# Packed rows loaded for two blocks by one transfer, maxima's transfers posted first, and mid-heads operand loads moved and spread, in a four-layer attention and Fourier network

## The chip, the cores and the metric

The kernel runs on one core of a Trainium2 chip. Its time is the device time of one execution in microseconds (us); for several runs the median is given. A core has five engines that work through their own instructions in order: PE (TensorE, matrix products; its weight loads are listed apart as PEld), DVE (VectorE), ACT (ScalarE), POOL (GpSimd) and SP (SyncE). Here SP issues every transfer (DMA), one after the other, and a transfer that has to wait holds up all that are behind it in SP's queue.

## The reference

Four layers are applied to x of 2048 rows by 640 columns: attention, Fourier, attention, Fourier.

```python
x = x + A(layernorm(x));  x = x + B(layernorm(x));  x = x + A(layernorm(x));  x = x + B(layernorm(x))
# A: 32 heads of 20 columns, sliding window of 256 keys, softmax, then @ wo
# B: Real(DFT over the sequence of (DFT over the columns))
```

All is float32; products are made from a high and a low part of each operand, three matrix products for one.

## The kernel before

**Heads stage.** The change lies in the attention layers, in `heads` (lines 522 to 743) and what it calls. Eight quads of four heads are worked through, each over 16 blocks of 128 rows. The loop runs over steps -10 to 128. In step t the scores of block s = t + 10 are made twice: first as rows, to find each row's maximum (`s_head`, PE L553, masked and reduced by DVE at L558), and ten steps later, for block t, transposed (`t_head`, PE L583, with the maximum subtracted by an extra row of the operand), exponentiated by ACT (L592) and masked by POOL (`t_mask`, L598 and L602). `pv` (PE L613) of block t - 1 comes at the end of step t and needs the masks of step t - 1. A step has two halves, z = 0 and z = 1.

**Maxima.** After each four blocks `m_rows` transposes their maxima (PE L565), ACT negates them into `mt` (L567), and two transfers (L569) put them into the extra rows of `qp`. That is at the end of every fourth step (86, 90, 94, 98); the first `t_head` that reads them comes at the start of the fourth step after it.

**Fill.** In the first half of each step PE also gets `fill`: matrix products for other parts of the layer (L191), first those that project x to queries and keys (`project`, `pieces`), and when these are done, the early part of the output projection (`partials`), which covers three of five operand chunks. 16 row tiles of it take two steps each. `more()` gives no fill while the first set of these operands, `early_o[0]`, is not complete. What is not done when the loop ends is done after it, at first tile by tile in `late`.

**Ticks.** Work on other engines that belongs to a later time is posted: `post(n, f)` runs f in the n-th tick from now, and each half step ends with a tick. Post 0 runs in the same tick as post 1, but before all that was posted for it. `defer(n, f)` runs f at the start of the n-th step from now. All this orders the program text only; what the engines do in time follows from their queues.

**Projected pieces.** A finished projection piece (128 columns of queries and keys, called chunk c, over 512 rows) is copied by ACT (L477), split by POOL (L478, L479) one and two ticks later, and stored to DRAM (`qk_d`, 512 KB) by `store_qk` (L456) six ticks after the copy. The last chunk is the tenth.

**Packed rows.** `pack(quad, sb)` loads a quad's rows from `qk_d` into `qp` and `kp` with 12 transfers of 20 rows by two groups by 512 columns (80 KB each, L510). It runs for four blocks at a time, eight steps ahead of their `s_head`, and three transfers go out at the start of each of four steps.

**Softmax sums.** `pv` also gives each row's sum. `finish` (L626 to L640) works on four finished blocks: at ticks 2, 12 and 14 it loads the sums back (`sm`, L631) and stores the outputs (L632), takes the reciprocal on DVE (L634) and stores it (L637).

**Early operands.** `prepare(2)` runs in step 84. It loads the first operand of the output projection (heads 0 to 15, chunk 0) by `load_o` (L759, and L765 for its scale). `others` waits, from step to step, until the reciprocals of quad 5's first four blocks are stored, and then loads the other two. Seven ticks after its load an operand is scaled by POOL (L782), four ticks later it is cut in two parts by ACT and POOL (L160, L166), and with the next tick it counts as complete. `prepare(4)`, after the last projection piece, in step 92, loads the first four row tiles of x (`load_y`, L853), one in each step. The sums of `partials` are added to them by DVE (L877).

Of the kernel before, what the change touches and what calls it, by code (L numbers as in the profile page):

```python
# [23 lines left out]
NQ = H // 4  # L24
NSB = 4
NB = S // P
NCH = 2 * D // P
# [36 lines left out]
class Net:  # L64
# [394 lines left out]
    def pieces(self, c, sbs, role):  # L459

        w = self.turn["w", c]
        sets, of = [], {}
        for sb in sbs:
            xt = self.xnt(sb)
            if sb % 2 == 0:
                sets.append(([], []))
            p = self.bank(role)
            of[id(p)] = p, sb, self.last_bank
            sets[-1][0].append(p)
            sets[-1][1].append([((w[:, 0, k, :], w[:, 1, k, :]), (xt[:, 0, k, :], xt[:, 1, k, :])) for k in range(KC)])  # L470

        lead = self.lead

        def copied(p, sb):
            st = self.work.tile([P, 2, 512], F32R, name="c", tag="c", bufs=3)
            r = self.raw()[:, :512]
            self.nc.scalar.activation(r, p, AF.Copy)  # L477
            self.post(1, lambda: self.nc.gpsimd.tensor_copy(st[:, 0, :], r))  # L478
            self.post(2, lambda: self.nc.gpsimd.tensor_tensor(  # L479
                out=st[:, 1, :], in0=r, in1=st[:, 0, :].bitcast(F32), op=OP.subtract))  # L480
            self.post(3 if lead else 6, lambda: self.store_qk(c, sb, st))
        for r in self.lockstep(sets):
            if isinstance(r, tuple):
                for p in r[1]:
                    p, sb, k = of[id(p)]
                    self.heavy.append((k, lambda p=p, sb=sb: copied(p, sb)))
                r = 0
            yield r
# [12 lines left out]
        self.prepare(4)  # L501


    def pack(self, quad, sb):

        todo = []
        cols = slice(sb * 512, (sb + 1) * 512)

        def put(d, src):
            self.nc.sync.dma_start(d.bitcast(F32), src)  # L510

        for kind in (1, 0):
            for e in range(2):
                r0 = 160 * quad + 80 * kind + 40 * e
                dst = (self.qp, self.kp)[kind][quad % 2].rearrange("p (z s) -> p z s", z=2)
                for part, l in enumerate(((0, 1, 0), (0, 0, 1))[kind]):
                    b = 64 * e + 20 * part
                    src = self.qk[l, r0:r0 + 40, cols].rearrange("(z r) s -> r z s", z=2)
                    todo.append(lambda d=dst[b:b + 20, :, cols], src=src: put(d, src))
        return todo  # L520

    def heads(self, xsrc, xdst, hook):
# [7 lines left out]
        def defer(d, fn):  # L530
            later.setdefault(now[0] + d, []).append(fn)
# [30 lines left out]
        def m_rows(quad, u):  # L562
            m = mc.pop((quad, u))
            p = self.banks[:16, s_bank(), :P]
            nc.tensor.transpose(p, m.rearrange("p z e j -> p (z e j)"), self.ident)  # L565
            mt = pool.tile([16, P], F32R, name="mt", tag="mt", bufs=1)
            nc.scalar.activation(mt, p, AF.Copy, scale=-1.0)  # L567
            for z in range(2):
                self.post(1, lambda z=z: nc.sync.dma_start(  # L569
                    qp[quad % 2][60:125:64, z, u * 512:(u + 1) * 512].bitcast(F32),  # L570
                    mt[8 * z:8 * z + 8, :].bitcast(F32)))

# [53 lines left out]
        def finish(quad, bk, ou):  # L626
            sm = pool.tile([P, 16], F32, name="sm", tag="sm")
            rc = pool.tile([P, 16], F32, name="rc", tag="rc")
            cols = slice(bk * 512, (bk + 1) * 512)
            at = (2, 12, 14) if quad < NQ - 1 else (1, 5, 6)  # L630
            self.post(at[0], lambda: nc.sync.dma_start(sm, ou[0:P:32, :]))  # L631
            self.post(at[0], lambda: nc.sync.dma_start(  # L632
                self.od[4 * quad:4 * quad + 4, :, cols].rearrange("h r s -> (h r) s"), ou))
# [2 lines left out]
            def store():  # L636
# [7 lines left out]
        done = [2 * NSB * per_piece]  # L644

        due = [(16 * q + 4 * j - AHEAD, ((-(-160 * (q + 1) // P) - 1) * NSB + 2 * (j // 2) + 2) * per_piece)
               for q in range(1, NQ) for j in range(NSB)]
        self.xsrc = xsrc
        self.out = self.partials(xsrc)
        self.rest = self.late(xsrc, xdst, hook)  # L650
# [44 lines left out]
        for step in range(-LEAD, steps + 1):  # L695
# [5 lines left out]
            if due and s >= due[0][0]:  # L701
                while done[0] < due[0][1]:
                    fill(15)
                due.pop(0)
                q, j = (s + AHEAD) // 16, (s + AHEAD) % 16 // 4
                for i, f in enumerate(self.pack(q, j)):
                    defer(i // 3, f)
                for f in later.pop(step, []):
                    f()
            if v >= 0 and v % 4 == 3:  # L710
# [100 lines left out]
    def prepare(self, n):  # L811
# [9 lines left out]
        elif n == 2:  # L821
# [11 lines left out]
            def others():  # L833

                if (CHUNKS[EARLY - 1][1] // 4 - 1, 0) not in self.stored:
                    self.defer(1, others)
                    return
                for k in range(1, EARLY):
                    self.early_o[0]["left"] -= 1
                    self.load_o(self.early_o[0], 0, k)  # L840
            self.defer(1, others)
        elif n == 4:
            self.take_big(2, F32)
            for i in range(AHEAD_X):
                if i == 0:
                    self.load_y([i])
                else:
                    self.defer(i, lambda i=i: self.load_y([i]))

    def load_y(self, ts):  # L850
        for t in ts:
# [878 lines left out]
```

## Time and profile before

| what | us |
|---|---|
| median of 3 runs (lowest, highest) | 2174.63 (2174.54, 2177.93) |
| the profiled execution: its own time | 2173.64 |
| its span, first to last instruction | 2171.9 |
| busy in the span: PE, DVE, ACT, POOL | 2116.4, 1611.6, 1167.9, 932.6 |
| first and last `s_head`, first attention layer to second | 125.0 to 1570.0 |
| mean granted clock of PE (1 is full) | 0.997 |

The profile is taken by the hardware from one execution. In its rows, "out<-in" names the tiles that an instruction writes and reads, L583 is line 583 of the kernel, and a bracket such as [0.44 <-POOL pt L598] is the idle time of the engine before the instruction with what ended it. A list of waits gives the engine and line that waited, what for, the total, the number of times and the longest. A queue name with a q (SPq) is the sequencer of that engine, which issues transfers. Engines that are not the bottleneck may idle for nothing.

### The profile page before, as it was taken

To read this page: it belongs to the slowest core of one execution; us is meant where nothing else is said; L and a number is where in the kernel's file an instruction comes from. 1 tells how busy PE (TensorE), PEld (TensorE's weight loads), DVE (VectorE), ACT (ScalarE), POOL (GpSimd) and SP (SyncE) were. 2 spreads that over 40 slices of the span, in tenths; PEclk is the share of its full clock that TensorE was granted. 3 is DMA by queue.
4 is the path that set the end of the run, shared out by engine and by line. 5 is a ranking of instruction groups with operands and counts; after the bars stand their busy time and mean duration, and the time that the engine had idled before them with its cause. 6 is when DMAs were issued, how large, how long until landed. Compare 5 with 4: busy or idle time off the path is not lost.

```text
span 2171.9 us, 49261 instructions
## 1 busy us (share of the span) xinstructions
PE 2116.4 (97%) x17893; PEld 1768.5 (81%) x17893; DVE 1611.6 (74%) x3933; ACT 1167.9 (54%) x2611; POOL 932.6 (43%) x1458
## 2 busy tenths in 40 slices
PE   7999999899999999999999999998999999999999
PEld 7987777687878888889999877776777788888899
DVE  6348888786897968787751578887768878688777
ACT  3117887766554545543431288786665545455522
POOL 3037777876514224230230477777754333242300
PEclk9999999999999999999999999999999999999999
DMA  5546666786435353657646466667853454546653
GB/s 184 177 146 198 203 190 212 218 233 200 135 122 180 132 187 126 224 196 258 214 140 189 152 201 187 207 193 224 233 184 130 130 189 136 165 148 218 221 176 125
DMA packets 221619, 395.41 MB, mean 182 GB/s; under 512 B 39360, under 2 KB 85952, under 8 KB 221376
## 3 DMA queue, kind: packets, MB, share of 16 engines
q1 hardware_dynamic: 221376, 392.26, 57.0%
q8 instruction: 141, 2.31, 0.5%
q14 instruction: 102, 0.84, 0.1%
HBM read 273.94 MB, written 117.05 MB: 180 GB/s over the span
## 4 chain that ended last, share of the span: by engine, by line
PE 81%; DVE 6%; POOL 4%; ACT 4%; DMA 3%; issue 2%; SPq 0%; ACTq 0%; POOLq 0%; DVEq 0%
PE banks L1269 27%; PE banks L173 14%; PE banks L191 13%; PE banks L613 8%; PE banks L1524 6%; PE banks L583 6%; PE banks L553 4%; POOL ou L1199 1%; POOL big L166 1%; DVE qp L166 1%; ACT big L931 1%; PE banks L273 1%; PE banks L565 1%; POOL rs L981 1%; ACT big L160 1%
## 5 line engine op out<-in xcount | busy, mean ns | idle before, releaser
L558 DVE CUSTOM_DVE_ANT_0 banks<-banks,mask 128x384 f32<-128x384 f32 (+2 forms) x1024 | 525.5, 559 | 153.4 <-PE banks L553 117.5
L592 ACT ACTIVATE pt<-banks 128x384 f32<-128x384 f32 (+2 forms) x1024 | 430.1, 472 | 139.8 <-PE banks L553 59.5
L583 PE MATMUL banks<-qp,kp 61*128 61x384 f32 (+2 forms) x1024 | 302.8, 365 | 9.7 <-DMA qp<-mt 7.7
L598 POOL TENSOR_SCALAR_AFFINE_SELECT pt<-pt 128x256 f32<-128x256 f32 x512 | 213.5, 418 | 174.9 <-ACT pt L592 128.4
L553 PE MATMUL banks<-kp,qp 60*128 60x384 f32 (+2 forms) x1024 | 279.1, 359 | 4.8 <-DVE mc L558 4.5
L191 PE MATMUL banks<-big,wc 64*128 64x512 f32 x1920 | 272.1, 394 | 0.4 <-DVE pt L374 0.4
L583 PEld LDWEIGHTS banks<-qp,kp 61*128 61x128 f32 x1024 | 176.8, 185 | 68.0 <-issue 27.4
L613 PE MATMUL banks<-pt,vq 128*32 128x128 f32 x5760 | 215.3, 277 | 4.4 <-POOL pt L598 4.4
L191 PEld LDWEIGHTS banks<-big,wc 64*128 64x128 f32 x1920 | 183.3, 185 | 29.1 <-ACT x L477 6.7
L613 PEld LDWEIGHTS banks<-pt,vq 128*32 128x32 f32 x5760 | 144.3, 109 | 65.2 <-issue 48.2
L1199 POOL TENSOR_TENSOR pt<-pt,pt 128x512 f32<-128x512 f32 x36 | 62.8, 1744 | 293.0 <-DMA pt<-c 188.3
L602 POOL TENSOR_SCALAR_AFFINE_SELECT pt<-pt 128x256 f32<-128x256 f32 x448 | 187.4, 418 | 0.0
L553 PEld LDWEIGHTS banks<-kp,qp 60*128 60x128 f32 x1024 | 163.7, 185 | 26.7 <-DVE mc L558 16.3
L160 ACT ACTIVATE c<-pt 128x512 fp32r<-128x512 f32 x150 | 93.5, 626 | 151.0 <-POOL pt L1175 52.4
L160 ACT ACTIVATE qp<-pt 128x512 fp32r<-128x512 f32 (+1 forms) x195 | 119.9, 624 | 92.2 <-DVE pt L1200 38.9
L166 DVE TENSOR_TENSOR c<-pt,c 128x512 fp32r<-128x512 f32 x150 | 125.0, 843 | 52.0 <-ACT c L160 49.8
L166 DVE TENSOR_TENSOR qp<-pt,qp 128x512 fp32r<-128x512 f32 (+1 forms) x195 | 150.2, 783 | 12.4 <-ACT qp L160 9.8
L1269 PE MATMUL banks<-qp,big 128*128 128x512 f32 x630 | 151.2, 391 | 4.9 <-DVE qp L166 3.9
L558 DVE DVE_READ_ACCUMULATOR2_ANT mc<- 128x1 f32 x1024 | 145.2, 142 | 0.0
L1269 PEld LDWEIGHTS banks<-qp,big 128*128 128x128 f32 x630 | 117.0, 188 | 31.0 <-DVE qp L166 5.6
L1269 PE MATMUL banks<-qp,xc 128*128 128x512 f32 x480 | 117.9, 390 | 1.5 <-DVE xc L166 1.2
L1269 PEld LDWEIGHTS banks<-qp,xc 128*128 128x128 f32 x480 | 89.8, 188 | 21.9 <-DVE xc L166 2.1
(224 smaller groups left out, 4388.6 us busy)
## 6 DMA issues: line engine op xcount, KB each, us to landing
pt<-c SPq DMA_DIRECT2D x188, 512.0 KB
qk_d<-c SPq DMA_DIRECT2D x80, 512.0 KB
kp<-qk_d SPq DMA_DIRECT2D x384, 80.0 KB
qp<-qk_d SPq DMA_DIRECT2D x384, 80.0 KB
kp<-u_d SPq DMA_DIRECT2D x32, 640.0 KB
o_d<-ou SPq DMA_DIRECT2D x64, 256.0 KB
x_d<-x SPq DMA_DIRECT2D x48, 320.0 KB
v_d<-pt SPq DMA_DIRECT2D x16, 768.0 KB
```

The source lines that it names most:

```text
L160: nc.scalar.activation(hi, src, AF.Copy, scale=-1.0 if neg else 1.0)
L166: (eng or nc.vector).tensor_tensor(out=lo, in0=src, in1=hi.bitcast(F32), op=OP.subtract)
L173: self.nc.tensor.matmul(p, x, y, start=n == 0, stop=n == last)
L191: self.nc.tensor.matmul(ps[a], x[r], y[r], start=half + i == 0, stop=half == 1 and i == n - 1, skip_group_check=True)
L553: nc.tensor.matmul(p, qp[quad % 2][b:b + 60, z, qb * P:(qb + 1) * P], kp[quad % 2][b:b + 60, z, k0 * P:(qb + 1) * P], start=True, stop=True)
L558: nc.vector.tensor_tensor_reduce(out=p, in0=p, in1=self.mask[:, 384 - n * P:], scale=1.0, scalar=NEG, op0=OP.add, op1=OP.max, accum_out=mc ...
L583: nc.tensor.matmul(self.banks[:, tb[e], :n * P], kp[quad % 2][b:b + 61, z, kb * P:(kb + 1) * P], qp[quad % 2][b:b + 61, z, kb * P:(kb + n) ...
L592: nc.scalar.activation(pt[quad, kb][:, 2 * z + e, :n * P], self.banks[:, tb[e], :n * P], AF.Exp, scale=SCALE)
L598: nc.gpsimd.affine_select(out=t[:, :, 0:P], in_=t[:, :, 0:P], pattern=[[0, 2], [1, P]], compare_op=OP.is_ge, fill=0.0, base=0, channel_mul ...
L602: nc.gpsimd.affine_select(out=t[:, :, 256:384], in_=t[:, :, 256:384], pattern=[[0, 2], [-1, P]], compare_op=OP.is_gt, fill=0.0, base=0, ch ...
L613: nc.tensor.matmul(p[32 * h:32 * h + 32, :], vq[:, 96 * (kb % 4) + 21 * h:96 * (kb % 4) + 21 * h + 32], t[:, h, (qb - kb) * P:(qb - kb + 1 ...
L1269: nc.tensor.matmul(self.banks[:, bk, :], p, b[q], start=start and m == 0, stop=stop and last and m == 2, skip_group_check=True)
```

## The change

Six edits, all of them in the heads stage of both attention layers:

- `pack` takes a number of quarters; in the loop it loads two (1024 columns, 160 KB a transfer), at the first and third of the four times, two transfers at the start of each of six steps.
- The maxima's transfers are posted with 0 instead of 1.
- The last chunk's pieces are stored eight ticks after their copy, not six.
- For quad 5's first four blocks the reciprocal and its store come at ticks 8 and 9, not 12 and 14.
- The second early operand is loaded three steps after `prepare(2)`; the third by `others`, which begins to look four steps after it, not one.
- The first four row tiles of x are loaded one, three, five and seven steps after `prepare(4)`, not zero to three.

```diff
--- before.py
+++ after.py
@@ -478,7 +478,7 @@
             self.post(1, lambda: self.nc.gpsimd.tensor_copy(st[:, 0, :], r))
             self.post(2, lambda: self.nc.gpsimd.tensor_tensor(
                 out=st[:, 1, :], in0=r, in1=st[:, 0, :].bitcast(F32), op=OP.subtract))
-            self.post(3 if lead else 6, lambda: self.store_qk(c, sb, st))
+            self.post(3 if lead else 6 if c < NCH - 1 else 8, lambda: self.store_qk(c, sb, st))
         for r in self.lockstep(sets):
             if isinstance(r, tuple):
                 for p in r[1]:
@@ -501,10 +501,10 @@
         self.prepare(4)
 
 
-    def pack(self, quad, sb):
+    def pack(self, quad, sb, n=1):
 
         todo = []
-        cols = slice(sb * 512, (sb + 1) * 512)
+        cols = slice(sb * 512, (sb + n) * 512)
 
         def put(d, src):
             self.nc.sync.dma_start(d.bitcast(F32), src)
@@ -566,7 +566,7 @@
             mt = pool.tile([16, P], F32R, name="mt", tag="mt", bufs=1)
             nc.scalar.activation(mt, p, AF.Copy, scale=-1.0)
             for z in range(2):
-                self.post(1, lambda z=z: nc.sync.dma_start(
+                self.post(0, lambda z=z: nc.sync.dma_start(
                     qp[quad % 2][60:125:64, z, u * 512:(u + 1) * 512].bitcast(F32),
                     mt[8 * z:8 * z + 8, :].bitcast(F32)))
 
@@ -628,6 +628,8 @@
             rc = pool.tile([P, 16], F32, name="rc", tag="rc")
             cols = slice(bk * 512, (bk + 1) * 512)
             at = (2, 12, 14) if quad < NQ - 1 else (1, 5, 6)
+            if (quad, bk) == (CHUNKS[EARLY - 1][1] // 4 - 1, 0):
+                at = (2, 8, 9)
             self.post(at[0], lambda: nc.sync.dma_start(sm, ou[0:P:32, :]))
             self.post(at[0], lambda: nc.sync.dma_start(
                 self.od[4 * quad:4 * quad + 4, :, cols].rearrange("h r s -> (h r) s"), ou))
@@ -644,7 +646,7 @@
         done = [2 * NSB * per_piece]
 
         due = [(16 * q + 4 * j - AHEAD, ((-(-160 * (q + 1) // P) - 1) * NSB + 2 * (j // 2) + 2) * per_piece)
-               for q in range(1, NQ) for j in range(NSB)]
+               for q in range(1, NQ) for j in range(0, NSB, 2)]
         self.xsrc = xsrc
         self.out = self.partials(xsrc)
         self.rest = self.late(xsrc, xdst, hook)
@@ -703,8 +705,8 @@
                     fill(15)
                 due.pop(0)
                 q, j = (s + AHEAD) // 16, (s + AHEAD) % 16 // 4
-                for i, f in enumerate(self.pack(q, j)):
-                    defer(i // 3, f)
+                for i, f in enumerate(self.pack(q, j, 2)):
+                    defer(i // 2, f)
                 for f in later.pop(step, []):
                     f()
             if v >= 0 and v % 4 == 3:
@@ -835,17 +837,17 @@
                 if (CHUNKS[EARLY - 1][1] // 4 - 1, 0) not in self.stored:
                     self.defer(1, others)
                     return
-                for k in range(1, EARLY):
-                    self.early_o[0]["left"] -= 1
-                    self.load_o(self.early_o[0], 0, k)
-            self.defer(1, others)
+                other(EARLY - 1)
+
+            def other(k):
+                self.early_o[0]["left"] -= 1
+                self.load_o(self.early_o[0], 0, k)
+            self.defer(3, lambda: other(1))
+            self.defer(4, others)
         elif n == 4:
             self.take_big(2, F32)
             for i in range(AHEAD_X):
-                if i == 0:
-                    self.load_y([i])
-                else:
-                    self.defer(i, lambda i=i: self.load_y([i]))
+                self.defer(1 + 2 * i, lambda i=i: self.load_y([i]))
 
     def load_y(self, ts):
         for t in ts:
```

## The prediction

> **What bounds the kernel now.** I read the page first (TensorE, PE, is busy for 97% of the span, so only the other 55 us can go), then the list of who waited for whom on PE, then a table of windows through the second attention layer, then the chain and the timeline where a window stood out. The waits on PE that the change can touch are two:
>
> ```profile
> PE banks L583 <- DMA qp<-mt: 7.7, 2, 4.8
> PE banks L613 <- POOL pt L598: 4.4, 7, 1.1
> ```
>
> Columns are total us, times, longest. The first is the exponent pass waiting for the maxima's transfer, once in each attention layer. The windows (bounds, length, then busy us of PE, PE's loads, DVE, ACT, POOL, then PE's clock, DMA share, GB/s) show an ordinary stretch, and those around the waits:
>
> ```profile
> 300.00:310.00 10.00, 10.00 (x149) 7.52 (x139) 7.10 (x32) 8.39 (x23) 9.77 (x20) 1.00 0.62 193
> 420.00:430.00 10.00, 6.59 (x68) 5.22 (x68) 5.14 (x21) 5.42 (x15) 7.27 (x14) 0.83 0.80 254
> 1490.00:1500.00 10.00, 8.51 (x117) 5.14 (x117) 8.28 (x32) 6.71 (x21) 8.00 (x18) 1.00 1.01 266
> 1500.00:1510.00 10.00, 5.18 (x51) 4.44 (x49) 3.18 (x14) 3.87 (x11) 4.89 (x9) 0.66 0.76 240
> ```
>
> In an ordinary stretch PE is full: fewer or later transfers there cannot shorten it, only lengthen it. Around the waits PE is idle, its granted clock drops, and the DMA engines are full (share 1.01) just before. The chain of work through that place in the second layer (start, us, what) goes through GpSimd (POOL) first and the maxima afterwards:
>
> ```profile
> 1486.16 1.27 POOL c L479
> 1487.43 0.55 POOL c L478
> 1487.98 0.37 POOL pt L598
> 1488.35 0.36 POOL pt L602
> 1488.71 1.27 POOL c L479
> 1489.97 0.37 POOL pt L598
> ...
> 1499.42 5.30 DMA qp<-mt
> ...
> 1510.22 1.32 PE banks L191 x18
> ```
>
> The timeline gives the steps (the first L583 of each) and both waits:
>
> ```profile
> 426.35 0.66 PE L583 MATMUL banks<-qp,kp 61*128 61x384 f32 x1 [2.87 <-DMA qp<-mt]
> 430.88 0.44 PE L583 MATMUL banks<-qp,kp 61*128 61x384 f32 x1
> 434.07 0.44 PE L583 MATMUL banks<-qp,kp 61*128 61x384 f32 x1
> 1493.27 0.32 PE L583 MATMUL banks<-qp,kp 61*128 61x128 f32 x1
> 1493.42 0.27 ACT L567 ACTIVATE mt<-banks 16x128 fp32r<-16x128 f32 x1
> 1495.59 0.44 PE L583 MATMUL banks<-qp,kp 61*128 61x384 f32 x1
> 1498.05 0.44 PE L583 MATMUL banks<-qp,kp 61*128 61x384 f32 x1
> 1504.86 0.66 PE L583 MATMUL banks<-qp,kp 61*128 61x384 f32 x1 [4.82 <-DMA qp<-mt]
> ```
>
> Counted from the stage's start these begin steps 98, 99, 100 of the first layer and 95, 96, 97, 98 of the second. The maxima of step 94 are ready at 1493.69, but SyncE's queue (SP) issues them only at 1499.42; the other transfers stand ahead of them there:
>
> ```profile
> 1488.02 1.33 SPq L759 DMA_DIRECT2D x<-o_d  x2
> 1492.31 0.34 SPq L853 DMA_DIRECT2D big<-x_d  x1
> 1495.15 0.37 SPq L456 DMA_DIRECT2D qk_d<-c  x1
> 1496.66 0.32 SPq L853 DMA_DIRECT2D big<-x_d  x1
> 1497.54 1.05 SPq L510 DMA_DIRECT2D kp<-qk_d  x3
> 1498.93 0.39 SPq L456 DMA_DIRECT2D qk_d<-c  x1
> ...
> 1501.41 0.35 SPq L853 DMA_DIRECT2D big<-x_d  x1
> ```
>
> **The change, part by part** (base: the profiled execution, 2173.64 us, of which 2171.9 are the span; the median of the runs is 0.99 higher).
>
> *Maxima first, loads and stores spread: the wait goes.* Post 0 runs in the same tick as post 1, only ahead of the others there. So it passes just the store in front (0.39 us of issue); most must come from the rest. Steps 92 and 93 lose both row loads (6 of 80 KB), step 92 its two operand loads and one scale load (768 KB), three of four x loads move behind step 94, and the last chunk's stores (512 KB each) fall behind the maxima. From step 92 to the maxima some 1.1 MB are issued instead of 3.6 MB, in a longer time. I take the whole wait as gone: -2.87 and -4.82.
>
> *Half clock after it.* Step 98 took 4.53 us in the first layer (426.35 to 430.88), the next, with the same work at full clock, 3.19. That is -1.34 in each layer with the wait. The Trainium skill ("TensorE: Matmul & The Clock Gate", Part 1) says the clock falls to half after an idle window of about 3.4 us and asks for no gap over about 3 us. Here the 2.87 us gap was followed by a window at 0.83, so the trace is stricter; by the page the first layer's 1.34 would not come from the wait, and the gain would be that much smaller.
>
> *Operands earlier: fill from step 95.* Scale values of quad 5 are stored at post 9 instead of 14, at the end of step 88 instead of in step 91. Operand 1 is loaded in step 87, operand 2 in step 89, both in 92 before. Scaling follows 7 ticks after a load, cutting 4 later, and the fill may start one tick after that: in step 95, not 98. Three steps without fill (95 to 97: 2.32 + 2.46 + 1.99, the last up to the wait) become three with fill at 3.19: +2.8. Each brings half a partial product forward, so that three late tiles run in the loop's last steps instead of behind it. Behind it one takes 1.70, as these two rows stand apart:
>
> ```profile
> 527.76 1.15 PE L173 MATMUL banks<-qp,kp 128*128 128x320 f32 x6 [0.42 <-DVE x L970]
> 529.45 1.14 PE L173 MATMUL banks<-qp,kp 128*128 128x320 f32 x6 [0.54 <-DVE x L970]
> ```
>
> That is -5.1; in the loop each takes the place of a fill of 18 matmuls (1.32 on the chain above), for which I charge the difference, 0.4, three times: +1.2. Net -1.1 (bounds 0, if Fourier's start is tied to something else, and -2).
>
> *The same operands on POOL.* Before, the scaling of two operands (step 95) and their cutting (step 97) were bursts of 2.5 us that cost PE nothing; POOL had idled before them:
>
> ```profile
> 1483.96 0.41 POOL L598 TENSOR_SCALAR_AFFINE_SELECT pt<-pt 128x256 f32<-128x256 f32 x1 [0.45 <-ACT pt L592]
> 1488.68 1.29 POOL L479 TENSOR_TENSOR c<-x,c 128x512 fp32r<-128x512 f32 x1
> 1490.39 0.41 PE L613 MATMUL banks<-pt,vq 128*32 128x128 f32 x4 [0.44 <-POOL pt L598]
> 1494.78 2.51 POOL L782 TENSOR_TENSOR x<-x,rr 128x512 f32<-128x512 f32 x2
> 1500.32 2.48 POOL L166 TENSOR_TENSOR big<-x,big 128x512 fp32r<-128x512 f32 x2
> ```
>
> Now operand 1 is scaled in step 90 (+1.25) and cut in step 92, and operand 2 is scaled in step 92 (+2.5 together), in the very tick that holds the last chunk's L479, ahead of the mask that the product of step 93 waits for. POOL is on the chain there and PE already waits 0.44 for that mask. Of the 3.75, 0.55 disappears in POOL's idle time ahead of 1484; the other 3.2 is added to PE's wait, which becomes 3.6 us. Upper bound 3.2; lower 0, if the burst were hidden as at 1494.78. I take 3.2, since the chain row shows no room; 0.2 for a shorter shortage in step 91. **The half clock** would follow this wait as it followed the old ones: between 0 (the window falls inside the wait) and 1.34; I take 0.9, since steps without fill need less of PE.
>
> *Packed rows by twos.* Twelve loads of 80 KB over four steps, twice, become twelve of 160 KB over six steps. Bytes are equal; 336 of 768 issues go, at 0.35 us each on SP (1.05 for three above), for which nobody waits in the ordinary window, so their end gains nothing. The last rows that a quad's first step needs now leave SP three steps ahead instead of five, and three steps (6.8 us even without fill) must hide issue and landing. The slowest landing among the rows above, behind a full queue, came 5.3 us after its issue, so I take 0; the upper bound is a rival below.
>
> *Sums' reciprocal four ticks earlier.* It waits on DVE for a transfer issued six ticks before it instead of ten; with the score reductions queued behind it, a late one would stop PE. In the last quad the same reciprocal follows after four ticks, and the answer for its line names no idle time of DVE ahead of any of the 64:
>
> ```profile
> L634 DVE RECIPROCAL rc<-sm x64: 189/248/253, 190.0 to 1609.0; 128x16 f32<-128x16 f32 x64
> ```
>
> Cost 0.
>
> *x loads.* Tile 3's addition comes three steps after its load instead of ten; at 3.19 a step that is 9.6 us. In the worst place of the profile a load (the fourth, 1501.41) was issued 8.1 us after its step's start at 1493.27. So between 0 and about 2 us per layer on DVE; I take 0, because the queue is shorter there until step 95.
>
> **Sum.** First layer: -2.87 - 1.34 - 1.1 + 3.2 + 0.2 + 0.9 = -1.0. Second: -4.82 - 1.34 - 1.1 + 3.2 + 0.2 + 0.9 = -3.0. Together -4.0: 2169.6 by the profiled execution, 2170.6 by the median; I say 2170.1.
>
> **Rivals.**
>
> *POOL's burst is hidden.* For it: the two 2.5 us bursts that cost nothing. Against: the chain through POOL. Then 4.3 less in each layer: 2161.5.
>
> *The wait only moves (slower).* What is taken from steps 92 to 94 is piled on steps 94 to 99: two chunk stores (1.0 MB), six pairs of packed loads (1.9), three x loads and three further tiles (1.9), the next block's operands (1.3), values and outputs (0.5): 6.3 to 6.6 MB, due by step 102, some 22.5 us later: about 285 GB/s. The best window above moved 266 at share 1.01. At that rate the last packed rows or the maxima of step 98 come 1 to 2 us late; at 240, as in the next window, some 4 us, with the half clock about 5 per layer: 2180. It decides from about 280 GB/s downwards; for less lateness the result is nearer 2173. The Trainium skill ("DMA: Bandwidth & Descriptors", on why a DMA increments its semaphore by 16) has a transfer from SP run on the largest number of engines up to 16 that divides the slowest dimension of both sides. By it the loads of 20 rows would use 10 engines, the 1.9 MB would fill those first, and the lateness would begin at a lower demand; no view here tells engines apart, and the numbers above do without it.
>
> *The change doesn't do what it says:* the maxima stay late although first in their tick, because SP itself is behind. Then step 98 still waits, but the transfers have gained the 3.2 us of POOL's wait: nothing is left in the first layer, 1.6 and the half clock in the second: 2170.6 + 2.9 = 2173.5, no difference.
>
> **How the numbers follow.** Forecast 0.50 (own range 2166 to 2175), hidden burst 0.18, wait moves 0.22, no effect 0.10. A measurement of this kernel tells 0.2% (4.3 us) from no change. Faster: half of the forecast and all of the hidden burst, 0.44. Slower: most of the moved wait, 0.18. Same: the rest, 0.38. The range that leaves out at most 2 in 10 reaches from the hidden burst, 2161, to short of the full moved wait, 2178.
>
> **What would show it.** Right: no wait for the maxima on L583; a wait of over 3 us on L613 for POOL's mask, about 10 us after the last projection fill, in both layers, with a clock dip; the first L191 of the partial products three steps earlier; the two-operand L782 and L166 gone as pairs. Wrong: that wait under 1 us (hidden), a wait of L553 or L583 for packed rows or maxima some 25 us later (moved), or PE idle anywhere in the ordinary stretch, which would mean that the packed rows come late at each quad.

## The result and the profile after

The changed kernel takes 2229.52 us (median of 5 runs, 2225.37 to 2231.59) against 2174.63: a ratio of 1.025 (95% interval 1.0239 to 1.0262). It is 55 us slower; the prediction said 4 us faster. The profiled execution has a span of 2223.7 us, 51.8 more than before. The list of who waited for whom on PE (total us, times, longest) shows new names:

```profile
PE banks L613 <- POOL pt L598: 16.0, 9, 4.3
...
PE banks L553 <- DMA vq<-v_d: 8.3, 3, 4.8
...
PE banks L553 <- DMA qp<-qk_d: 5.3, 2, 4.6
...
PE banks L553 <- DMA big<-x: 2.9, 1, 2.9
PE banks L553 <- DMA o_d<-ou: 2.1, 1, 2.1
...
PE banks L583 <- DMA qp<-mt: 1.9, 1, 1.9
PE banks L553 <- DMA r_d<-rc: 1.8, 1, 1.8
```

The wait of L583 for the maxima has all but gone. L553, the first product of a block, now waits for transfers; before, it waited for none. The transfer behind the arrow is not to be relied on here. All transfers share eight semaphores (counters by which one engine tells another that something is done; more of them in the last section), and the name is that of the transfer whose semaphore moved last. L553 reads only the packed rows. By the landings in the trace (the last semaphore update of each transfer) a row load is what ends each of these eight waits: the last one landed 0.1 to 0.4 us before L553 started. The load behind the wait named `o_d`, for example, left SP at 416.19 and landed at 422.67; L553 started at 423.02. So the 20.4 us of these waits are all waits for packed rows. The windows (columns as in the prediction), first three after the change, then the first layer's steps 92 to 102 in the kernel before:

```profile
300.00:310.00 10.00, 10.00 (x155) 7.47 (x153) 7.10 (x31) 8.51 (x22) 9.75 (x20) 1.00 0.69 172
420.00:430.00 10.00, 7.74 (x75) 5.53 (x75) 3.74 (x14) 3.75 (x12) 3.99 (x9) 0.57 0.53 128
411.56:466.58 55.02, 40.88 (x479) 30.97 (x475) 27.32 (x101) 24.82 (x65) 30.72 (x56) 0.78 0.77 186
```

```profile
408.41:443.77 35.36, 30.44 (x425) 22.23 (x421) 25.36 (x97) 22.85 (x62) 25.62 (x50) 0.95 0.81 231
```

The third line is the same steps 92 to 102 after the change: 55.0 us instead of 35.4. In that time the transfers move less per us (186 GB/s, not 231), so the DMA engines are not simply full. The timeline of PE names the large waits there:

```profile
419.80 0.64 PE L613 MATMUL banks<-pt,vq 128*32 128x128 f32 x4 [3.13 <-POOL pt L598]
...
423.02 0.66 PE L553 MATMUL banks<-kp,qp 60*128 60x384 f32 x1 [2.08 <-DMA o_d<-ou]
...
450.10 0.64 PE L613 MATMUL banks<-pt,vq 128*32 128x128 f32 x4 [3.34 <-POOL pt L598]
461.30 0.67 PE L553 MATMUL banks<-kp,qp 60*128 60x128 f32 x2 [4.64 <-DMA qp<-qk_d]
...
493.38 0.78 PE L553 MATMUL banks<-kp,qp 60*128 60x384 f32 x2 [2.87 <-DMA big<-x]
```

They fall in steps 93, 94, 100, 102 and 110. Steps 94, 102 and 110 are the ones whose block (step + 10 = 104, 112, 120) is the first to need a new pair of row loads. The chain of work through this place runs from landing to issue to landing:

```profile
429.68 5.71 DMA kp<-qk_d
...
435.41 8.51 DMA kp<-qk_d
...
443.94 9.30 DMA big<-x
...
453.58 7.48 DMA qp<-qk_d
...
461.30 0.67 PE banks L553 x2
```

A row load issued at 435.41 lands 8.51 us later, and only then does SP issue the next x load, at 443.94. Why that one, SP's timeline tells (x2 is two issues):

```profile
435.41 1.58 SPq L510 DMA_DIRECT2D kp<-qk_d  x2
438.17 0.34 SPq L537 DMA_DIRECT2D vq<-v_d  x1
438.96 0.53 SPq L761 DMA_DIRECT2D x<-o_d  x1
440.45 0.52 SPq L767 DMA_DIRECT2D rr<-r_d  x1
441.01 0.59 SPq L855 DMA_DIRECT2D big<-x  x1
441.65 0.74 SPq L510 DMA_DIRECT2D qp<-qk_d  x2
443.94 0.36 SPq L855 DMA_DIRECT2D big<-x  x1
```

Count the issues: the one at 443.94 is the eighth behind the one at 435.41. The chain's step from 429.68 to 435.41 also spans eight issues, and so does the one from 443.94. SP has eight transfers under way and waits with the ninth until the first has landed. So it is with all 1548 issues of this trace: none goes out before the transfer eight places ahead has landed. Transfers that land late therefore hold up everything behind them, x loads, maxima and values alike.

Where the 51.8 us came from, by the starts of the steps (first L583 of each) against before:

| steps | first layer | second layer |
|---|---|---|
| up to 92 (ordinary stretch) | +3.5 | +1.9 |
| 93 (POOL's mask) | +2.9 | +4.1 |
| 94 to 96 | +5.8 | +6.7 |
| 97 and 98 (old waits for maxima) | -3.2 | -5.2 |
| 99 to 102 | +14.0 | +12.6 |
| 103 to 126 | +6.4 | +4.7 |

The sum is 54.2; outside these steps 2.4 come back. The 3.34 us on L613 in step 100 also go back to a late transfer: POOL stands still for a scale transfer, and the masks are queued behind it (POOL's timeline).

```profile
448.43 1.26 POOL L784 TENSOR_TENSOR x<-x,rr 128x512 f32<-128x512 f32 x1 [4.56 <-DMA rr<-r_d]
```

### The profile page after: what moved, and what is told of

The parts are those of the page before. It is cut to its first block, busy times and chain, and to the rows that moved or that the text cites. A ratio compares the mean times of both kernels' runs of the same rounds, so it can differ in the third digit from the quotient of the medians.

```text
span 2223.7 us, 48932 instructions
## 1 busy us (share of the span) xinstructions
PE 2136.1 (96%) x17929; PEld 1786.6 (80%) x17929; DVE 1610.4 (72%) x3933; ACT 1170.4 (53%) x2611; POOL 925.1 (42%) x1458
## 4 chain that ended last, share of the span: by engine, by line
PE 75%; DVE 8%; DMA 7%; ACT 4%; POOL 3%; issue 2%; SPq 1%; ACTq 0%; DVEq 0%; POOLq 0%
PE banks L1271 27%; PE banks L173 14%; PE banks L191 12%; PE banks L613 7%; PE banks L1526 6%; PE banks L583 5%; PE banks L553 3%; DMA qp<-qk_d 2%; DVE qp L166 1%; DMA kp<-qk_d 1%; POOL ou L1201 1%; DMA r_d<-rc 1%; DMA vq<-v_d 1%; ACT pt L592 1%; DVE st L218 1%
## 5 line engine op out<-in xcount | busy, mean ns | idle before, releaser
L583 PE MATMUL banks<-qp,kp 61*128 61x384 f32 (+2 forms) x1024 | 311.2, 369 | 4.0 <-DMA qp<-mt 1.9
L553 PE MATMUL banks<-kp,qp 60*128 60x384 f32 (+2 forms) x1024 | 279.4, 363 | 26.3 <-DMA vq<-v_d 8.3
L598 POOL TENSOR_SCALAR_AFFINE_SELECT pt<-pt 128x256 f32<-128x256 f32 x512 | 210.8, 412 | 220.8 <-ACT pt L592 167.2
L613 PE MATMUL banks<-pt,vq 128*32 128x128 f32 x5760 | 218.7, 280 | 16.0 <-POOL pt L598 16.0
L583 PEld LDWEIGHTS banks<-qp,kp 61*128 61x128 f32 x1024 | 180.7, 188 | 63.4 <-ACT pt L592 23.3
L613 PEld LDWEIGHTS banks<-pt,vq 128*32 128x32 f32 x5760 | 145.6, 110 | 78.7 <-issue 47.8
L553 PEld LDWEIGHTS banks<-kp,qp 60*128 60x128 f32 x1024 | 164.2, 189 | 50.0 <-issue 21.6
L602 POOL TENSOR_SCALAR_AFFINE_SELECT pt<-pt 128x256 f32<-128x256 f32 x448 | 183.7, 410 | 0.0
L166 DVE TENSOR_TENSOR c<-pt,c 128x512 fp32r<-128x512 f32 x158 | 132.8, 846 | 28.9 <-ACT c L160 27.9
L160 ACT ACTIVATE c<-pt 128x512 fp32r<-128x512 f32 x158 | 98.6, 624 | 87.6 <-DVE pt L1202 27.2
```

The lines of the kernel that those rows point to most:

```text
L160: nc.scalar.activation(hi, src, AF.Copy, scale=-1.0 if neg else 1.0)
L166: (eng or nc.vector).tensor_tensor(out=lo, in0=src, in1=hi.bitcast(F32), op=OP.subtract)
L553: nc.tensor.matmul(p, qp[quad % 2][b:b + 60, z, qb * P:(qb + 1) * P], kp[quad % 2][b:b + 60, z, k0 * P:(qb + 1) * P], start=True, stop=True)
L583: nc.tensor.matmul(self.banks[:, tb[e], :n * P], kp[quad % 2][b:b + 61, z, kb * P:(kb + 1) * P], qp[quad % 2][b:b + 61, z, kb * P:(kb + n) ...
L598: nc.gpsimd.affine_select(out=t[:, :, 0:P], in_=t[:, :, 0:P], pattern=[[0, 2], [1, P]], compare_op=OP.is_ge, fill=0.0, base=0, channel_mul ...
L602: nc.gpsimd.affine_select(out=t[:, :, 256:384], in_=t[:, :, 256:384], pattern=[[0, 2], [-1, P]], compare_op=OP.is_gt, fill=0.0, base=0, ch ...
```

## The experiments

Each kernel is the one before with the edits named. Medians (of 4 to 11 runs) are in us. The ratio to before, with its 95% interval, is that of the record and not the quotient of two medians. In the diffs, which show the lines that matter, `...` marks what is left out.

| edits | median | ratio |
|---|---|---|
| rows by twos, as in the change | 2201.33 | 1.0143 (1.0116 to 1.0169) |
| everything but the rows | 2192.74 | 1.0082 (1.0066 to 1.0098) |
| rows by twos in four steps | 2194.78 | 1.0104 (1.0082 to 1.0125) |
| the rows' six steps, 80 KB each | 2201.44 | 1.0125 (1.0110 to 1.0140) |
| rows by twos in six steps, two sooner | 2188.25 | 1.0065 (1.0050 to 1.0081) |
| rows by twos in eight steps, four sooner | 2179.93 | 1.0030 (1.0018 to 1.0042) |
| maxima first, stores and x loads spread | 2173.69 | 1.0000 (0.9992 to 1.0009) |
| operands' move | 2186.13 | 1.0053 (1.0040 to 1.0066) |
| all but rows, fill held to step 98 | 2180.71 | 1.0031 (1.0020 to 1.0043) |
| all but rows, fill held to step 96 | 2179.26 | 1.0019 (1.0010 to 1.0028) |
| operands set apart, fill held to 98 | 2177.27 | 1.0016 (1.0007 to 1.0025) |
| the same, stores and x loads as before | 2175.65 | 1.0008 (0.9999 to 1.0016) |
| spread, operands in steps 90 and 92 | 2177.06 | 1.0019 (1.0010 to 1.0028) |
| the same, stores and x loads as before | 2175.93 | 1.0009 (1.0000 to 1.0018) |
| whole change, rows in eight steps, fill held to 96 | 2187.50 | 1.0062 (1.0046 to 1.0077) |
| before, eight x loads left out | 2165.96 | 0.9952 (0.9935 to 0.9969) |

**The rows.** The theory after the result was that the packed rows are the cause; the rival, the prediction's own, that the other transfers moved into steps 94 to 99 are.

```diff
...
-                for i, f in enumerate(self.pack(q, j)):
-                    defer(i // 3, f)
+                for i, f in enumerate(self.pack(q, j, 2)):
+                    defer(i // 2, f)
```

> Before, with only the packed rows changed (two blocks by one transfer of 160 KB, over six steps). Theory A (the rows: each such transfer takes 5 to 9 us from issue to landing, holds SP's queue up, and ends too late for its step): most of the loss is here, 30 us or more, so 2205 to 2225 us, with waits of PE on L553 for DMA in steps 94, 102 and 110. Theory B (the rival of the prediction: the other transfers moved into steps 94 to 99 make the pile): the rows alone cost little, 2175 to 2182 us.

The run without them undoes exactly this:

> The changed kernel with the rows loaded as before (80 KB, one block at a time, over four steps). Theory A: what the prediction summed for the other edits holds, so 2168 to 2176 us, with PE waiting some 3 us on L613 for POOL in step 93 and no wait of L583 for the maxima. Theory B: the pile stays, 2195 us or more, with waits of PE for DMA in steps 94 to 102.

2201.33 and 2192.74: the rows alone cost 27.5 us, all the rest 18.9. Neither theory holds by itself. Together the two make 46.4 of the 54.9; whether the other 8.5 appear only with both is open, since the interval of the rows' ratio alone is some 6 us wide to each side. In the rows' run L553 waits for rows in steps 78, 102 and 110 of both layers; step 94, which the first theory named as well, has no such wait. L583 waits for maxima in steps 98 and 102 (list of waits, first layer; `x<-o_d` is again a row load that ended a wait):

```profile
PE banks L583 <- DMA qp<-mt: 5.7, 2, 3.3
PE banks L553 <- DMA qp<-qk_d: 3.9, 3, 2.3
PE banks L553 <- DMA x<-o_d: 3.5, 1, 3.5
```

Is it the size of the transfers, their lateness, or their crowding? Four runs vary these. The first diff is against the run just shown, the next two against the kernel before, the last against the third run:

```diff
-                    defer(i // 2, f)
+                    defer(i // 3, f)
```

> Before, with rows by 160 KB, but three a step over four steps, so that the last leave SP five steps ahead of their use, not three. If lateness of the issue is the cause: nearly all comes back, 2172 to 2182 us. If the transfer's size is the cause (slow landing, SP held up): still 2195 us or more, and near the first run of this call.

```diff
...
+                for i, (f, g) in enumerate(zip(self.pack(q, j), self.pack(q, j + 1))):
+                    defer(i // 2, f)
+                    defer(i // 2, g)
```

> Before, with the rows' schedule of the change (the bytes of two blocks over six steps), but each 160 KB transfer replaced by its two halves of 80 KB, issued one behind the other: the same bytes in the same steps, 24 issues more per pair of blocks. If lateness is the cause: as slow as the first run of this call, 2200 us or more. If the transfer's size is: 2173 to 2185 us.

```diff
...
+        due = sorted((16 * q + 4 * j - AHEAD - 2 * (q > 1), ((-(-160 * (q + 1) // P) - 1) * NSB + 2 * (j // 2) + 2) * per_piece, q, j)
+                     for q in range(1, NQ) for j in range(0, NSB, 1 if q == 1 else 2))
...
+                for i, f in enumerate(self.pack(q, j, 1 if q == 1 else 2)):
+                    defer(i // 3 if q == 1 else i // 2, f)
```

> Before, with the change's rows over six steps, but two steps sooner from the second quad on, so that the last leaves SP five steps ahead. If lateness is what the six-step form lost by: 2174 to 2184 us. If it is crowding (320 KB a step instead of 240): 2188 to 2202 us, with waits of L583 for maxima.

```diff
-        due = sorted((16 * q + 4 * j - AHEAD - 2 * (q > 1), ((-(-160 * (q + 1) // P) - 1) * NSB + 2 * (j // 2) + 2) * per_piece, q, j)
+        due = sorted((16 * q + 4 * j - AHEAD - 4 * (q > 1), ((-(-160 * (q + 1) // P) - 1) * NSB + 2 * (j // 2) + 2) * per_piece, q, j)
...
-                    defer(i // 3 if q == 1 else i // 2, f)
+                    defer(i // 3 if q == 1 else 2 * i // 3, f)
```

> Before, with rows by 160 KB, but as many bytes in a step as before and as early: from the second quad on, the twelve transfers of two blocks go out over eight steps that begin four steps sooner, so that the last still leaves SP five steps ahead of its use (the first quad is loaded as before). If the size of a transfer is what costs: 2185 us or more. If lateness (six steps) and crowding (four steps) are what cost, and the size nothing: 2172 to 2179 us.

In the change's six steps 80 KB loses as much as 160 KB (2201.44 against 2201.33): for the time, the size hardly matters there. The landings do differ: from 160 to 400 us a load of 160 KB lands 5.6 us after its issue in the median, one of 80 KB in the same steps 3.8, before 3.4. Four steps are on time and still lose 21 us, now through the maxima, which travel among more rows: they land 4.4 us after their issue in the median of the same stretch, before 2.5 (list of waits, whole span, in an execution of 2203.09 us; before it was 7.7, 2, 4.8):

```profile
PE banks L583 <- DMA qp<-mt: 19.8, 8, 4.8
```

Six steps two steps sooner win 13.1 back and end where crowding was expected to (2188.25, with L583 waiting for maxima); eight steps four sooner win another 8.3; about 6 remain. So the cause is both: too late, and too many bytes a step. (In these last two the first quad that the loop loads, the second of eight, is loaded as before, which may be part of the gain.) What remains is again waits for maxima, first layer and second, where before they are 2.9 and 4.8:

```profile
PE banks L583 <- DMA qp<-mt: 5.8, 2, 4.5
PE banks L583 <- DMA qp<-mt: 9.3, 4, 5.1
```

Of these, 1.25 and 2.50 us fall in step 18, behind steps 10 to 13, in which by the code the last loads of the old schedule and the first of the earlier one go out together. For the rest, size and earlier start are not separated.

**The other edits.** First the maxima, stores and x loads by themselves:

```diff
...
-                self.post(1, lambda z=z: nc.sync.dma_start(
+                self.post(0, lambda z=z: nc.sync.dma_start(
...
+            self.post(3 if lead else 6 if c < NCH - 1 else 8, lambda: self.store_qk(c, sb, st))
...
+                self.defer(1 + 2 * i, lambda i=i: self.load_y([i]))
```

> Before, with the maxima posted first, the last chunk stored two ticks later and the x loads spread; rows and operands as before. By the prediction's sum the two waits for maxima and their half clock go and nothing takes their place: 2174 - 10.4 = 2163 to 2166 us. If the wait only moves: 2172 to 2177 us.

2173.69: nothing. The waits for maxima in step 98 are gone (0.9 us of waiting for ACT is left there), and one of 2.0 to 2.2 us comes up four steps later, at the next maxima. In the second layer, step 102:

```profile
1517.63 0.41 PE L583 MATMUL banks<-qp,kp 61*128 61x384 f32 x1 [2.19 <-DMA qp<-mt]
```

This is the rival of the prediction in its mild form, for which it said "nearer 2173". Then the operands:

```diff
...
-            self.defer(1, others)
+                other(EARLY - 1)
...
+            self.defer(3, lambda: other(1))
+            self.defer(4, others)
```

> Before, with the operands' move alone (second one loaded in step 87, third in 89, sums' reciprocal four ticks sooner). If the operands' move carries the loss of the run without the rows: 2190 to 2200 us, with PE waiting some 3 us on L613 for POOL in step 93, half clock after it, and longer steps from 99 to 117. If the loss there came from transfers spread into those steps: 2174 to 2180 us.

2186.13: 12.4 us lost, under the expected 2190, with the wait, the half clock and the long steps where they were expected. To part POOL's wait from the early fill, the fill is held back in the run without the rows:

```diff
-            if not made[0] and self.early_o[0]["left"]:
+            if not made[0] and (self.early_o[0]["left"] or now[0] < 98):
```

> The run without the rows, with the partial products held back to step 98, where they start before; operands loaded, scaled and cut as early as in the change. If the 18.9 us that it lost are POOL's wait in step 93 with its half clock (2.9 + 2.8 in a layer, less the waits for maxima): 2176 to 2182 us, and steps 99 to 117 as in the kernel before. If they are something else that the early loads do: 2188 to 2194 us still.

> The run without the rows, with the fill held back to step 96 instead of 95 (nothing) or 98. If the fill's early start costs by the number of steps it comes early: between the two, 2186 to 2190 us. If it costs by where the next operands' scaling and cutting fall against other transfers and masks, the size is open; a value within 2 us of one of the two (2181 or 2193) would speak for it.

A start in step 95, 98 and 96 gives 2192.74, 2180.71 and 2179.26. Starting the fill two steps early costs nothing that these runs show; starting it three early costs 12 us. So the cost does not grow step by step. By the profiled executions it lies in steps 99 to 117: with a start in 95 they take 6.6 and 7.4 us longer than before (first and second layer), in 96 1.9 and 2.9, in 98 0.3 and 1.5 less. With the start in 95 the next block's operands are loaded, scaled and cut three steps sooner as well, and a row tile, which takes two steps, begins in an odd step; 96 and 98 are both even. Steps 99, 101, 109, 111, 115 and 117 are each 0.7 to 1.0 us longer than before in both layers. A start in step 97, which would tell whether it is the odd step or the three steps, was not tried. In the largest single loss that follows, 2.6 us in step 107 of the first layer (3.4 in the second), POOL stands still for a late scale transfer with the masks queued behind it (POOL's timeline, then PE's, of the run without the rows):

```profile
465.79 2.51 POOL L784 TENSOR_TENSOR x<-x,rr 128x512 f32<-128x512 f32 x2 [3.32 <-DMA rr<-r_d]
468.25 0.41 POOL L598 TENSOR_SCALAR_AFFINE_SELECT pt<-pt 128x256 f32<-128x256 f32 x1
```

```profile
468.71 0.41 PE L613 MATMUL banks<-pt,vq 128*32 128x128 f32 x4 [1.51 <-POOL pt L598]
```

The scale transfer left SP at 459.45 and landed at 465.65. Why it is late at 95 and not at 96 was not settled. The run with the fill held to 98 shows the clock after POOL's wait, in steps 95, 96 and 97:

```profile
418.41:421.86 3.45, 3.27 (x33) 2.09 (x32) 2.17 (x8) 1.37 (x6) 0.81 (x2) 0.50 0.58 186
421.86:425.36 3.50, 3.39 (x38) 2.10 (x34) 2.17 (x8) 2.02 (x5) 1.45 (x4) 0.50 0.96 280
425.36:428.00 2.64, 2.53 (x22) 1.31 (x18) 1.89 (x7) 1.99 (x5) 0.84 (x3) 0.50 0.74 255
```

Half clock stays until the fill comes. Next the operands are kept off the tick of the last chunk's splitting, first on both sides of it (loads in steps 86 and 91, fill held to 98), then behind it (90 and 92; here the reciprocal stays at ticks 12 and 14, and the fill is not held). In all four runs the maxima are posted first. The diffs show the operands' loads against the operands' move:

```diff
-            self.defer(3, lambda: other(1))
-            self.defer(4, others)
+            self.defer(2, lambda: other(1))
+            self.defer(7, others)
```

> The run with the fill held back to step 98, with the second operand loaded one step earlier and the third two steps later, so that neither is scaled or cut in the tick of the last chunk's splitting. If the wait in step 93 comes from that pile on POOL: it falls back to some 0.4 us, the half clock of steps 94 to 97 goes, and with the waits for maxima gone as well the time is 2164 to 2170 us. If freeing POOL only brings the waits for maxima back (the transfers lose the 3 us of POOL's stall): 2172 to 2177 us.

> The same, with the x loads and the last chunk's stores where they are before. If the wait for maxima hangs on all that goes out between steps 92 and 94, it is back in part: 2168 to 2174 us, with a wait on L583 in step 98. If the two operand loads in step 92 were enough to cause it: the same as the run without the step-98 wait, 2164 to 2170 us.

```diff
+            self.defer(6, lambda: other(1))
+            self.defer(8, others)
```

> Maxima posted first, the last chunk stored later, x loads spread; of the early operands the second is loaded in step 90, the third in 92, so that POOL scales and cuts both behind the last chunk's splitting. If that pile was what cost the operands' move: the wait in step 93 is 0.4 us as before and no half clock follows in steps 94 to 97. With half of the transfers of step 92 gone the wait for maxima in step 98 should go; if nothing takes its place 2164 to 2169 us, if it moves to step 102 as in the run with the spread alone 2172 to 2176 us.

> The same with the x loads and the last chunk's stores where they are before. If the wait for maxima of step 98 needs both operand loads in step 92: 2164 to 2169 us, without a wait in steps 98 and 102. If the rest of the pile is enough: about 2174 us, with the wait in step 98 as before.

None gains. On both sides of the splitting, POOL's wait in step 93 falls from 3 to 1.40 us, but the half clock in steps 95 to 97 stays as in the rows above, and no wait for maxima returns; that PE's slow steps give the transfers their time is likely and was not tried. Behind it, POOL's wait is back at 0.42 and the clock stays full in steps 94 to 97, and the waits for maxima are back: with the spread in step 102 of both layers (and 1.2 us in 98 of the second), without it in step 98 (5.5 and 3.8 us). From the start of step 92 to that of 103 these orders take 35.4 to 38.7 us, against 35.4 and 37.4 before. So either the order is immaterial because the amount of transfers sets the time, or a good order was missed. Taking transfers out decides:

```diff
-                self.nc.sync.dma_start(self.y_part(t), self.xsrc[t * P:(t + 1) * P, :])
+                if t < 8:
+                    self.nc.vector.memset(self.y_part(t), 0.0)
+                else:
+                    self.nc.sync.dma_start(self.y_part(t), self.xsrc[t * P:(t + 1) * P, :])
```

> Before, with the loads of the first eight row tiles of x (320 KB each, in steps 92 to 106) left out: VectorE fills these tiles with zeros instead, so x is missing from those rows' sums. If the amount of transfers sets the time from step 92 to 103: both waits for maxima go and nothing takes their place, 2162 to 2168 us. If it is the order (what stands ahead of the maxima in SP's queue), four x loads of 0.35 us each are too little to matter: 2171 us or more.

2165.96, 9 us less: both waits for maxima are gone, and no other wait for a transfer takes their place. In the profiled execution steps 92 to 102 of the first layer take 32.9 us. In the second they take 37.6, no less than before: there VectorE, which here also writes the zeros, keeps L553 waiting for 0.7 us in step 93 and 0.6 in step 94, as in the first layer, but in the second half clock follows, for 17.07 us. This execution took 2171.93 us; the other three, with a mean clock of 0.999 to 1.000, took 2164.70 to 2166.54. So what goes out sets the time, more than its order. Whether the bytes count or the number of transfers (each keeps one of eight places until it lands) is not separated: this run leaves out both. The last run puts the found causes together:

> The whole change with two things set right: rows (160 KB) over eight steps, four steps sooner, from the second quad on, and the fill held back to step 96. If the causes found are all: the fill at 96 gave 2179, the rows over eight steps +6, so 2181 to 2189 us, 40 us or more below the changed kernel. If the parts do something together that has not been seen: 2200 us or more.

2187.50, within the expected interval: the rows' steps and the fill's start account for 42 of the 55 us. What is left shows in its lists of waits as POOL's mask in step 93 (3.12 and 3.43 us) and the maxima (8.7 us in all).

## Why the prediction was wrong

**The step that failed is "Packed rows by twos ... I take 0".** It saw that the last rows leave SP three steps ahead instead of five, held 6.8 us of cover against a slowest landing of 5.3 us, and found no cost. Measured alone: 27.5 us. Two things failed. The first is the cover: a row load takes up to 8.51 us to land (the chain above), and SP waits meanwhile. The 5.3 us came from one 4 KB transfer in a full queue, no measure of several 160 KB loads one behind the other; even the loads of 80 KB took up to 6.4 us in steps 92 to 102 of the kernel before. The second was not asked: 320 KB go out in a step instead of 240, and the maxima travel among them. With the last issue as early as before (six steps, two sooner) some 14.5 of the 27.5 us stay.

**The rival "the wait only moves" had the mechanism** (rows and maxima late in steps 94 to 102) and the wrong size. It set demand against 266 and 240 GB/s and came to 2180 by the latter; with eight transfers under way the stretch moved 186 GB/s. It also reckoned one wait of 4 us in each layer; there were three to four, each with half clock around it, for 3.4 to 13.7 us.

**The waits for maxima and their half clock** (-2.87, -4.82, -1.34 twice) went as forecast: -3.2 and -5.2 in steps 97 and 98, after the longer fill steps. But taking the wait "as gone" left out where the bytes go: in the run with this edit alone they stop PE in step 102, and the net is 0.0.

**Operands earlier.** The fill did start in step 95. Steps 95 to 97, for which 2.8 us were charged, cost 3.0 and 3.8 us in the two layers of the changed kernel, the half clock in step 95 included. The term of -5.1 for three late tiles in the loop failed: in the run without the rows the time from the start of step 127 to the next layer's first `s_head` fell from 683.92 to 683.52 us (from these rows of before, then of that run):

```profile
518.33 0.33 PE L583 MATMUL banks<-qp,kp 61*128 61x128 f32 x2
...
1202.25 0.33 PE L553 MATMUL banks<-kp,qp 60*128 60x128 f32 x2
```

```profile
528.97 0.36 PE L583 MATMUL banks<-qp,kp 61*128 61x128 f32 x2
...
1212.49 0.33 PE L553 MATMUL banks<-kp,qp 60*128 60x128 f32 x2
```

By the code, the late tiles wait for the last quad's sums, however early the partial products end; that was argued, not tried. And what follows from a start in step 95 rather than 96 or 98, 12 us, was not priced at all; which of its followers costs so much is in part open (above).

**POOL's wait** was right: 3.6 us forecast, 3.13 and 4.28 measured, in step 93, for the reason given: POOL scales one operand, cuts another and splits the last chunk ahead of the mask (POOL's timeline, changed kernel).

```profile
415.67 1.28 POOL L784 TENSOR_TENSOR x<-x,rr 128x512 f32<-128x512 f32 x1
416.89 1.27 POOL L166 TENSOR_TENSOR big<-x,big 128x512 fp32r<-128x512 f32 x1
418.11 1.27 POOL L479 TENSOR_TENSOR c<-x,c 128x512 fp32r<-128x512 f32 x1
419.33 0.42 POOL L598 TENSOR_SCALAR_AFFINE_SELECT pt<-pt 128x256 f32<-128x256 f32 x1
```

The half clock behind it was mis-sized: 0.9 us a layer forecast; in the run without the rows step 94 took 1.24 longer than before and step 95 4.78 us where a filled step at full clock takes 3.19, so 2.8. The prediction thought that thin steps need less of PE; they do, but they also keep the clock down.

**The reciprocal** cost nothing, as said: the answer for its line again names no idle time of DVE ahead of it. **The x loads**, for which 0 was taken of 0 to 2 us, came late in the changed kernel, where DVE's additions wait for them (the list of waits on DVE):

```profile
DVE big L879 <- DMA big<-x: 4.5, 1, 4.5
DVE big L879 <- DMA big<-x_d: 2.4, 1, 2.4
```

In the run with the spread alone no such wait is listed: the lateness comes with the held queue, not with the spread alone.

## What to carry to other kernels

When a stretch is held by transfers, ask first how much must land in it, and only then in what order; here five orders gave 2173.7 to 2177.3 us, none better than before, and half of the x loads left out gave 9 us. Bigger or fewer transfers must leave the queue as early as the small ones did: compare the last issue with the first use, and take landing times from loads of the same size in the same company. Work that is brought forward brings its own followers forward too; price where these fall on the other engines.

## What the runs showed of the hardware

**Eight under way.** In the traces of all eighteen kernels SP's transfers use eight semaphores in a fixed turn, and no issue starts before the transfer eight places ahead of it, which has the same semaphore, has landed; the shortest time between the two is 16 ns. SP's instructions carry this wait for the semaphore that they then hand to their own transfer. So the limit is one of the program as it was built, with eight semaphores; whether the queue itself would take more, no run shows. It binds where landings are slow: 255 of 1884 issues before and 315 of 1548 after the change go out within 0.15 us of that landing, and 438 of 1548 with the rows in four steps.

**The same bytes cost more DMA time in larger rows.** From 160 to 400 us the kernel before and the one with the rows alone moved 202 GB/s each, at a DMA share of 0.65 and 0.75:

```profile
160.00:400.00 240.00, 237.34 (x3364) 176.96 (x3364) 195.56 (x737) 189.35 (x499) 181.94 (x394) 1.00 0.65 202
```

```profile
160.00:400.00 240.00, 235.72 (x3332) 175.46 (x3332) 193.27 (x731) 187.87 (x494) 178.55 (x390) 1.00 0.75 202
```

With the rows' schedule at 80 KB it was 0.69 at 200 GB/s, so a part of the difference goes with the schedule. That 20 rows use 10 engines, as the Trainium skill has it ("DMA: Bandwidth & Descriptors", on why a DMA increments its semaphore by 16), agrees with the traces: each of the 768 row loads before and the 432 after the change moves its semaphore eleven times, once soon after its issue (in the median 0.5 us) and ten times as it lands, where a load of 128 rows moves it sixteen times.

**A short wait is enough for the half clock when the work around it is thin.** In the run with the operands on both sides of the splitting, step 93 (1.40 us of waiting), 94 and 95:

```profile
411.39:415.55 4.16, 2.47 (x37) 1.40 (x33) 2.27 (x10) 2.00 (x5) 4.16 (x8) 1.00 0.80 188
415.55:418.44 2.89, 2.62 (x36) 1.43 (x35) 2.27 (x9) 1.79 (x6) 2.89 (x6) 0.84 0.87 212
418.44:421.89 3.45, 3.27 (x33) 2.09 (x32) 2.17 (x8) 1.35 (x6) 1.29 (x4) 0.50 0.59 186
```

The Trainium skill ("TensorE: Matmul & The Clock Gate", Part 1) has the clock fall after an idle window and rise again after some 3.4 us of sustained work, by a window that runs free of the program. The traces agree with the window: from 100 to 2100 us of all eighteen traces each of the 70 stretches of half clock lasts 3.41 us or a whole multiple of it, up to seven times. In the kernel before it is one from the end of the first layer's wait for maxima on (426.08 to 429.49) and two around the second's (1501.28 to 1508.11). They agree with the rise (half clock ends with the first dense steps), and with the chance in it: in the run without eight x loads, step 95 kept full clock in the first layer and had lost it in the second, after waits of 0.7 us in step 93 and 0.6 in step 94 of both:

```profile
418.98:421.59 2.61, 2.07 (x33) 1.34 (x33) 2.54 (x10) 1.42 (x6) 1.48 (x3) 1.00 0.89 311
```

```profile
1493.32:1496.77 3.45, 3.27 (x33) 2.09 (x32) 2.22 (x9) 1.37 (x6) 2.13 (x3) 0.50 0.90 333
```

The trace is stricter on the fall: 1.40 us of waiting was enough, where the page (section "Why this matters for your kernels") asks for no gap over about 3 us.
